# The last three c-rows of w_down: two loads of 96 partitions and five small ones in place of two loads of 128

## The chip, the cores and the metric

The kernel runs on one core of a Trainium2 chip. The metric is the device time of one execution in microseconds; the number given is the median of several runs.

## What is computed

One decode step of a transformer block for a single token: a layer norm, grouped-query attention against a long cache (32 query heads, 4 key and value heads, 65536 cached positions, head size 128), a residual, then a second layer norm and a gated feed-forward layer (model width D = 1024, F = 3584), again with a residual. All tensors are bfloat16.

```python
def _A_ref(x, k_cache, v_cache, wq, wo):
    q = (x @ wq)                      # 32 heads of 128
    scores = einsum(q, k) * Dh ** -0.5
    o = einsum(softmax(scores), v)
    return o @ wo
def _B_ref(x, w_gate, w_up, w_down):
    return (gelu(x @ w_gate) * (x @ w_up)) @ w_down
h  = x + _A_ref(layernorm(x), k_cache, v_cache, wq, wo)
h2 = h + _B_ref(layernorm(h), w_gate, w_up, w_down)
```

(cut: reshapes, transposes and the repeat of the key and value heads are left out.)

## The kernel before

The kernel reads some 173 MB once: the weights and the two caches. Everything is streamed through one large buffer in SBUF, `ring` (128 partitions, five chunks of 32 KB each per partition). `load` at L160 picks the next chunks and issues one DMA on SP's queue (L167); all large loads go this way, in the order of the program. The small input row x is loaded on ACT's queue at L172, four partitions of 512 bytes. SP waits before a load until the chunk it overwrites has been used. A later load can thus be queued on the DMA engines while earlier ones are still running.

The order of the loads is: wq (two), the 16 key and 8 value loads of the attention, wo (two), w_gate (one), w_up (two), and w_down (five). Helpers `pe`, `dv` and `ac` keep the order of the instructions on TensorE, VectorE and ScalarE as written; matmuls are all recorded under L145 or L147, which are lines of the helper `mm`.

The change touches the last stage. `w_down` (3584 x 1024) is seen as `wd_v`, 128 partitions of 28 rows c of 1024 values: partition p holds the rows 28p to 28p + 27 of the matrix, so c counts the rows inside a partition. The 28 c-rows are loaded in five pieces of `sizes = [14, 7, 4, 2, 1]` c-rows (L538), all side by side in `ring`, so that the last piece, 256 KB, is small. After each piece come its matmuls: for each c four (`out_mm`, L467), one for each quarter of the 1024 columns, with the padded activation column `actz[:, c, :]` as the stationary operand and 256 columns of the weights as the moving one, all summed into `f_ps`. Those four run in four column groups of TensorE. `keep_busy` (L543) adds matmuls into an unused bank between the pieces, 3, 2 and 1 after the first three.

```python
for sz, nb in zip(sizes, busy):
    at[0] = 0
    wv = load(wd_v[:, c0:c0 + sz, :], c0 * D)
    for cc in range(sz):
        c = c0 + cc
        out_mm(actz[:, c, :], lambda g: wv[:, cc, g * OW:(g + 1) * OW], False, c + 1 == FC)
```

At the end VectorE copies `f_ps` to `o_fin` as bfloat16 (L558), and SP stores it, four partitions of 512 bytes (L559).

Of the kernel before, what the change touches and what calls it, by code (L numbers as in the profile page):

```python
# [17 lines left out]
def kernel(  # L18
# [13 lines left out]
    nc = tc.nc  # L32
    P = 128
    D = A_x.shape[-1]
# [6 lines left out]
    FC = F // P  # L41
# [35 lines left out]
    ring = chpool.tile([P, NBUF * CW], BF16, name="ring")  # L77
# [80 lines left out]
    at = [0]  # L158

    def load(src, off=0):  # L160
        n, w = src.shape[1], src.shape[2]
        units = -(-(off + n * w) // CW)
        o = at[0] * CW + off
        assert o + n * w <= NBUF * CW
        at[0] = (at[0] + units) % NBUF
        tv = ring[:, o:o + n * w]
        nc.sync.dma_start(out=tv.rearrange("p (n w) -> p n w", w=w), in_=src)  # L167
        return tv.rearrange("p (n w) -> p n w", w=w)
# [23 lines left out]
    for bp in range(4):  # L192
        s0 = 64 * (bp // 2) + bp % 2
        nc.vector.tensor_copy(out=esel[:, bp, :, :],
                              in_=ident_bf[:, s0:s0 + 63:2].unsqueeze(1).to_broadcast([P, 4, 32]))
# [27 lines left out]
    def padded(pool, vec, ncols, name, tag=None):  # L223
        t = pool.tile([P, ncols, 32], BF16, name=name, tag=tag or name)
        nc.gpsimd.memset(t[:], 0.0)
        nc.vector.tensor_copy(out=t[:, :, 0], in_=vec)
        return t
# [228 lines left out]
    for wc in range(Hq // WN):  # L456
        wv = load(wo_v[:, wc * WN:(wc + 1) * WN, :])
        for cc in range(WN):
            c = wc * WN + cc
# [7 lines left out]
    def out_mm(stat, mov, first, last, groups=range(4)):  # L467
        for g in groups:
            mm(f_ps[32 * g:32 * g + 32, :], stat, mov(g), first, last, tile_position=(0, 32 * g),
               skip_group_check=True)  # L470
# [65 lines left out]

    wd_v = B_w_down.rearrange("(p c) n -> p c n", p=P)
    sizes = [14, 7, 4, 2, 1]  # L538
    assert sum(sizes) == FC
    actz = padded(rows, act_bf[:], FC, "actz")  # L540
    w_ps = row_bank("w_ps")

    def keep_busy(n, src):  # L543
        for _ in range(n):
            mm(w_ps[:], ident_bf[:], src, True, True)

    keep_busy(8, wu[:, 0, 0:512])
    busy = [3, 2, 1, 0, 0]
    c0 = 0
    for sz, nb in zip(sizes, busy):  # L550
        at[0] = 0
        wv = load(wd_v[:, c0:c0 + sz, :], c0 * D)
        for cc in range(sz):
            c = c0 + cc
            out_mm(actz[:, c, :], lambda g: wv[:, cc, g * OW:(g + 1) * OW], False, c + 1 == FC)
        c0 += sz
        keep_busy(nb, wv[:, 0, 0:512])
# [32 lines left out]
```

## Time and profile before

| what | value |
|---|---|
| median of 3 runs | 408.42 us (408.33 to 408.43) |
| span of the profiled execution | 406.9 us |
| DMA on SP's queue (q1) | 173.02 MB, 98.7% of 16 engines' span |
| bytes read, over the span | 173.02 MB, 425 GB/s |
| TensorE matmuls | 293.1 us busy, 72% |
| VectorE | 202.7 us busy, 50% |
| ScalarE, GpSimd | 44.7 us (11%), 7.4 us (2%) |
| mean granted TensorE clock | 0.912 |

The profiled execution's own time is its span, from the first to the last instruction of the core; the time of a run also has what lies around it, and the median of the runs is 1.5 us above the span. On a profile's page the rows of digits show the busy share in 40 equal slices, in tenths. In the chain that ended last each step is followed back to what released it. In a timeline, each row has the start and the duration in microseconds, the engine, the line of the kernel, the operation, out<-in, the shape and how many instructions were merged; the brackets give the idle time of the engine before them and what ended it. Names on DMA queues: q1 carries the kernel's loads from SP, q10 the load of x from ACT, q8 and q14 fetches of instructions.

### The profile page before, as it was taken

What the parts mean: (1) busy time and instruction counts of PE and PEld (TensorE: products, weight loads), DVE (VectorE), ACT (ScalarE), POOL (GpSimd) and SP (SyncE); (2) the same over time, 40 slices, a digit from 0 to 9 for tenths busy, and PEclk for the clock granted to TensorE, in tenths of its full rate; (3) what the DMA queues carried; (4) which work ended last, traced back from release to release, by engine and by line L of the source; (5) the groups of instructions that cost most, each with busy time, mean ns of one, the idle gap of its engine ahead of it and who ended that gap; (6) DMA issues with size and microseconds to landing.
All of it is one profiled execution on the core that took longest, in us unless ns stands there. A gap on an engine that the chain in (4) does not pass through costs nothing.

```text
span 406.9 us, 2667 instructions
## 1 busy us (share of the span) xinstructions
PE 293.1 (72%) x1495; PEld 60.8 (15%) x743; DVE 202.7 (50%) x185; ACT 44.7 (11%) x67; POOL 7.4 (2%) x17
## 2 busy tenths in 40 slices
PE   1346777769977699597776979976597969636283
PEld 0011111111111112111110111111111101212031
DVE  1118899955978359147971880879433000220110
ACT  1010000022000040100000420000041000100000
POOL 2000000000000000000000000000100000100000
PEclk9986899987989999899996998999989899886889
DMA  9999999999999999999999999999999999999995
GB/s 367 457 412 448 427 419 461 413 444 424 415 464 419 409 499 414 393 438 425 490 414 403 448 425 435 417 457 432 445 438 432 433 399 435 445 436 414 437 419 222
DMA packets 5213, 173.19 MB, mean 426 GB/s; under 512 B 585, under 2 KB 593, under 8 KB 849
## 3 DMA queue, kind: packets, MB, share of 16 engines
q1 hardware_dynamic: 5192, 173.02, 98.7%
q8 instruction: 9, 0.15, 0.1%
q14 instruction: 4, 0.02, 0.0%
q10 hardware_dynamic: 8, 0.00, 0.0%
HBM read 173.02 MB, written 0.00 MB: 425 GB/s over the span
## 4 chain that ended last, share of the span: by engine, by line
DMA 53%; PE 31%; DVE 12%; ACT 2%; issue 0%; SPq 0%; ACTq 0%
DMA ring<-in_A_v_cache_dram 31%; PE acc_ps L147 11%; DVE ring L281 9%; PE qk_ps L145 7%; DMA ring<-in_A_k_cache_dram 7%; DMA ring<-in_B_w_down_dram 7%; DMA ring<-in_B_w_gate_dram 7%; PE qk_ps L147 7%; PE acc_ps L145 4%; DVE mx L302 2%; ACT sc L301 2%; PE wg_ps L145 0%; PE wg_ps L147 0%; DVE pT L330 0%; ACT pe_r L327 0%
## 5 line engine op out<-in xcount | busy, mean ns | idle before, releaser
L281 DVE STREAM_TRANSPOSE ring<-ring 128x2048 uint32<-128x2048 uint32 x64 | 142.7, 2280 | 33.6 <-DMA ring<-in_A_k_cache_dram 33.5
L145 PE MATMUL qk_ps<-ring,wsel 128*128 128x512 bf16 x256 | 100.8, 394 | 35.8 <-DVE mx L302 23.6
L147 PE MATMUL acc_ps<-ring,pT 128*128 128x512 bf16 x384 | 114.1, 409 | 0.0
L147 PE MATMUL qk_ps<-ring,wsel 128*128 128x512 bf16 x256 | 100.6, 393 | 0.0
L145 PE MATMUL acc_ps<-ring,pT 128*128 128x512 bf16 x128 | 52.7, 412 | 20.4 <-DMA ring<-in_A_v_cache_dram 17.6
L145 PEld LDWEIGHTS <-wsel 128*128 128x128 bf16 x256 | 25.4, 99 | 135.1 <-issue 134.4
L301 ACT COPY sc<-qk_ps 128x1024 f32<-128x1024 f32 x16 | 16.2, 1011 | 176.8 <-PE qk_ps L147 176.7
L302 DVE TENSOR_REDUCE mx<-qk_ps 128x1 f32<-128x1024 f32 x16 | 19.6, 1222 | 26.0 <-ACT sc L301 26.0
L145 PEld LDWEIGHTS <-pT 128*128 128x128 bf16 x128 | 13.3, 104 | 119.1 <-issue 113.2
L357 DVE COPY acc_sb<-acc_ps 32x512 f32<-32x512 f32 x8 | 5.4, 672 | 36.6 <-PE acc_ps L147 36.6
L327 ACT ACTIVATE pe_r<-sc,nbias 128x1024 bf16<-128x1024 f32 x16 | 18.2, 1140 | 39.2 <-DVE nbias L322 38.5
L330 DVE STREAM_TRANSPOSE pT<-pe_r 128x1024 bf16<-128x1024 bf16 x16 | 19.0, 1226 | 6.2 <-ACT pe_r L327 6.2
L359 ACT COPY acc_sb<-acc_ps 32x512 f32<-32x512 f32 x8 | 4.6, 577 | 65.0 <-DVE acc_sb L357 65.0
L145 PE MATMUL q_ps<-ring,xnz 128*32 128x512 bf16 x32 | 5.2, 623 | 7.9 <-DMA ring<-in_A_wq_dram 7.9
L145 PE MATMUL wu_ps<-ring,hnz 128*32 128x512 bf16 x32 | 4.7, 503 | 7.8 <-DMA ring<-in_B_w_up_dram 7.8
L145 PE MATMUL wg_ps<-ring,hnz 128*32 128x512 bf16 x32 | 4.6, 517 | 7.7 <-DMA ring<-in_B_w_gate_dram 7.7
L145 PE MATMUL ln_tot<-ln_s,ones_f 128*128 128x1 f32 x8 | 1.9, 312 | 10.8 <-DVE ln_s L199 9.0
L315 DVE TENSOR_REDUCE gm<-mxT_ps 1x8 f32<-1x128 f32 x4 | 1.1, 279 | 16.1 <-PE mxT_ps L156 16.1
L145 PE MATMUL o_ps<-sel,acc_sb 128*128 128x8 f32 x32 | 4.2, 257 | 6.5 <-DVE rl L371 5.7
L145 PE MATMUL f_ps<-ring,actz 128*32 128x256 bf16 x112 | 4.0, 274 | 4.8 <-DMA ring<-in_B_w_down_dram 4.8
L237 DVE COPY q_ev<-q_ps 128x512 f32<-128x512 f32 x1 | 0.7, 692 | 13.3 <-PE q_ps L147 13.3
L237 DVE COPY wg_ev<-wg_ps 128x512 f32<-128x512 f32 x1 | 0.7, 691 | 11.6 <-PE wg_ps L145 11.6
(103 smaller groups left out, 89.2 us busy)
## 6 DMA issues: line engine op xcount, KB each, us to landing
ring<-in_A_k_cache_dram SPq DMA_DIRECT2D x16, 4096.0 KB, 33.9
ring<-in_A_wq_dram SPq DMA_DIRECT2D x2, 4096.0 KB, 16.5
ring<-in_A_wo_dram SPq DMA_DIRECT2D x2, 4096.0 KB, 30.8
ring<-in_B_w_gate_dram SPq DMA_DIRECT2D x1, 7168.0 KB
ring<-in_B_w_up_dram SPq DMA_DIRECT2D x2, 3584.0 KB, 30.5
ring<-in_B_w_down_dram SPq DMA_DIRECT2D x1, 3584.0 KB, 37.1
ring<-in_B_w_down_dram SPq DMA_DIRECT2D x1, 1792.0 KB
ring<-in_B_w_down_dram SPq DMA_DIRECT2D x1, 1024.0 KB, 29.3
```

Source lines behind the costliest of these rows:

```text
L145: return pe(t.matmul(out, lhsT=lhsT, rhs=rhs, start=start, stop=stop, tile_position=tile_position, skip_group_check=skip_group_check))
L147: op = t.add_instruction(mybir.InstMatmult(name=nc.get_next_instruction_name(), engine=t.engine, start_tensor_calc=start, stop_tensor_calc ...
L237: nc.vector.tensor_copy(out=dst, in_=src)
L281: dv(nc.vector.transpose(out=kt[:, c * w:(c + 1) * w], in_=kt[:, c * w:(c + 1) * w]))
L301: ac(nc.scalar.copy(out=sc[:], in_=flat))
L302: dv(nc.vector.tensor_reduce(out=state[("mx", g)][:, li:li + 1], in_=flat, axis=AX.X, op=ALU.max))
L315: dv(nc.vector.tensor_reduce(out=gm[:], in_=mxT_ps[:].rearrange("o (x h) -> o h x", h=rep), axis=AX.X, op=ALU.max))
L327: ac(nc.scalar.activation(out=pe_r[:], in_=state.pop(("sc", g, li))[:], func=ACT.Exp, bias=nbias[:, 0:1], scale=scale, accum_out=lpart[:, ...
L330: dv(nc.vector.transpose(out=pT[:].rearrange("p m c -> p (m c)"), in_=pe_r[:]))
L357: dv(nc.vector.tensor_copy(out=acc_sb[sl, :], in_=acc[sl, c, :]))
L359: ac(nc.scalar.copy(out=acc_sb[sl, :], in_=acc[sl, c, :]))
```

## The change

The first three loads of w_down (14, 7 and 4 c-rows) stay. The last two (2 and 1 c-rows) are cut to the partitions 0 to 95. The partitions 96 to 127 get their last three c-rows together, 6 KB a partition, in five loads of 12, 8, 6, 4 and 2 partitions. All ten loads are issued ahead of the first matmul of the stage in the program; the matmuls, their order and `keep_busy` stay. The places in `ring` stay the same too. The matmuls of the last two pieces read all 128 partitions, so they now depend on the five small loads also.

```diff
-    assert sum(sizes) == FC
+    shared = [96, 96]
+    extra = [12, 8, 6, 4, 2]
+    assert sum(sizes) == FC and 96 + sum(extra) == P
...
     c0 = 0
+    wd_s = ring[:, 0:FC * D].rearrange("p (c n) -> p c n", n=D)
+    ends = FC - sum(sizes[3:])
+
+    def wd_load(p0, p1, ca, cb):
+        nc.sync.dma_start(out=wd_s[p0:p1, ca:cb, :], in_=wd_v[p0:p1, ca:cb, :])
+
+    for sz, rows_in in zip(sizes, [P, P, P] + shared):
+        wd_load(0, rows_in, c0, c0 + sz)
+        c0 += sz
+    p0 = shared[0]
+    for n in extra:
+        wd_load(p0, p0 + n, ends, FC)
+        p0 += n
+    c0 = 0
     for sz, nb in zip(sizes, busy):
-        at[0] = 0
-        wv = load(wd_v[:, c0:c0 + sz, :], c0 * D)
+        wv = wd_s[:, c0:c0 + sz, :]
```

## The prediction

> **What bounds the kernel now.** I read the page first: which resource is full, and what the chain that ended last is made of.
>
> ```profile
> DMA  9999999999999999999999999999999999999995
> DMA 53%; PE 31%; DVE 12%; ACT 2%; issue 0%; SPq 0%; ACTq 0%
> q1 hardware_dynamic: 5192, 173.02, 98.7%
> q8 instruction: 9, 0.15, 0.1%
> q14 instruction: 4, 0.02, 0.0%
> ```
>
> The loads on q1 keep the 16 DMA engines busy for 98.7% of the span; PE and DVE steps of the chain lie beside loads that are under way. So the end is set by the last bytes of the last loads, and by what follows them. The end of the merged chain of waits shows that tail:
>
> ```profile
> 373.51 29.95 DMA ring<-in_B_w_down_dram
> 403.51 0.32 PE f_ps L145 x4
> 403.85 0.42 DVE o_fin L558
> ```
>
> The last load is issued at 373.51 and lands just before 403.51; then four matmuls, one copy, the store. The timeline shows what each of the five w_down loads (14, 7, 4, 2, 1 rows of c) releases:
>
> ```profile
> 395.00 1.71 PE L145 MATMUL f_ps<-ring,actz 128*32 128x256 bf16 x56 [1.63 <-DMA ring<-in_B_w_down_dram]
> 399.24 0.95 PE L145 MATMUL f_ps<-ring,actz 128*32 128x256 bf16 x28 [1.78 <-DMA ring<-in_B_w_down_dram]
> 401.67 0.62 PE L145 MATMUL f_ps<-ring,actz 128*32 128x256 bf16 x16 [0.94 <-DMA ring<-in_B_w_down_dram]
> 402.89 0.40 PE L145 MATMUL f_ps<-ring,actz 128*32 128x256 bf16 x8 [0.28 <-DMA ring<-in_B_w_down_dram]
> 403.51 0.29 PE L145 MATMUL f_ps<-ring,actz 128*32 128x256 bf16 x4 [0.21 <-DMA ring<-in_B_w_down_dram]
> 404.30 0.66 SPq L559 DMA_DIRECT2D out_dram<-o_fin  x1
> ```
>
> Groups of 16, 8 and 4 take 0.62, 0.40 and 0.29 us: 0.0275 us for each matmul more. The eight of the fourth load are over before the fifth lands.
>
> **Which engine is late, and why.** The arrivals on the last load's semaphore, one for each DMA engine, run from 401.55 to 403.46: the engines end 1.9 us apart. The trace's packet records have start, duration and bytes, but no engine. They can still be followed: on one engine the next packet starts 4 ns before the recorded end of the last, and every engine has the same list of sizes. Followed this way, the records fall into sixteen complete chains. Their last markers (4 bytes, some 0.32 us before the arrival) lie at: four chains at 401.22, 401.44, 401.53 and 401.81, without any fetch of code; eight at 402.51 to 403.14, with one 16 KB fetch each (the q8 line: eight of its nine fetches fall in before the end); and four that also carried the four-row load of x at the start, at 401.32, 401.39, 402.11 (one 8 KB fetch of q14) and 403.06 (two such fetches). A 16 KB fetch sets its engine back by some 1.4 us (955 ns of its own, and 481 more for the packet beside it, 1694 instead of 1213), an 8 KB fetch by 0.84 us (309 + 530).
>
> So there is something to even out: the mean of the sixteen ends is 402.35, the last 403.14.
>
> **The change, part by part.** Packets of 2, 4 and 8 KB follow each other at 80, 155 and 306 ns, so one of 6 KB costs some 230, and 236 with its marker. Rows 0 to 95 in 16 equal shares are 6 rows instead of 8 for each engine: 2 x (155 + 80) = 0.47 us less. Rows 96 to 127 then go one row to an engine: 12 + 8 + 6 + 4 + 2 = 32. The trace has one load of few rows, that of x: four rows, four engines, four arrivals (6.92 to 7.04). I read from it that a load of n rows takes n engines, and that the same first ones come first. [...]
>
> At full pace the balance is then: engines with no extra row -0.47; one, -0.23; two, 0.00; three, +0.24; four, +0.47; five, +0.71. The four chains that carried x are the ones with four or five. One of these is the chain that ended at 403.06. It began its last three rows of c at 403.06 - 8 x 0.235 - 0.01 = 401.17; now it has 6 x 0.235 = 1.41 shared and 0.94 or 1.18 of extras, and ends at 403.52 or 403.76. The eight late chains go forward to 402.9 and below, for nothing: the last marker moves from 403.14 to 403.5 or 403.8, +0.38 or +0.62.
>
> What a packet costs where several engines write to few neighbouring rows, no row of the trace shows: every large load goes to 128 rows at once. Below, the bound is the same pace: packets from 2 to 64 KB all run at it, so I exclude a gain. Above, I take double, somewhat over the dearest sharing that the trace has: a fetch beside a load's packet makes 1694 of 1213 (x 1.40), and 955 of some 608 (x 1.57). I take x 1.4, the row that is nearest to two streams that meet: the small loads put up to twelve engines on twelve adjacent rows while the late engines still write there, and the shared ones 16 on 96. The late low engine then ends at 401.17 + 1.97 + 1.32 = 404.46 or + 1.65 = 404.79: +1.32 or +1.65. Doubled, it is 401.17 + 2.82 + 1.89 or 2.36 = 405.9 or 406.35.
>
> [...]
>
> **PE.** In the changed program's order the first weight load of the fourth group waits for all five small loads and the 96-row load with it. So 12 matmuls (0.51 us by the step of 0.0275) instead of 4 (0.29) follow the last landing: +0.22. Behind them stand only the copy and the store. Gaps of 1.63 and 0.21 us before a group leave the step per matmul the same, so a longer gap costs no pace. Waiting on six counters instead of one costs between 0 and 0.1 us; I take 0.
>
> **SP.** Five issues more, of 0.33 to 0.43 us, on a queue with nothing else left but the store: "SPq L559 <- DVE o_fin L558" waited 30.3 us. They reuse arrival counters, so the loads of 8, 6, 4 and 2 rows are issued only after the two w_up loads and the first two w_down loads have landed: 377.96, 386.41, 394.95 and 399.20. The store's first packet came 1.26 us after its issue began (404.30 to 405.56), so the two-row load can start at 400.5; the earliest low engine is free for it at 401.32 - 0.47 + 3 or 4 x 0.236 = 401.6 or later. Covered by 1.1 us; without that cover it would be added one for one.
>
> **Sum.** Against the profiled execution (span 406.9; the median of the runs, 408.42, is 1.5 above it, for what lies around the span): +1.32 or +1.65 from the last marker, +0.22 from PE: +1.5 to +1.9. Predicted: 408.42 + 1.7 = 410.1.
>
> **Rivals.**
> *Full pace.* Packets to few rows run as before. Then +0.38 or +0.62, and 0.22: 409.0 to 409.3. For it: the one pace of all packets. Against it: 32 rows in small loads is a layout that the trace doesn't have.
> *Not slower.* The low engine that ends late gets at most two of the five extra rows (n x 0.236 below 0.47), because small loads are dealt over other engines than x was. Then the last marker is a late chain with one extra row, 403.14 - 0.23 = 402.90, and with 0.22 of PE the sum is 408.4. The most that evening out could ever bring is 403.14 - 402.35 = 0.79, less 0.22: 407.85. From the trace: for it, that eight of the nine late ends belong to chains which x did not use; against it, the ninth.
> *Doubled packets.* +2.7 to +3.2 and 0.22: 411.4 to 411.9.
>
> **How the numbers follow.** Forecast, with sharing between 1.2 and 1.9 times: 0.50. Full pace: 0.27. Not slower: 0.18. Doubled or worse: 0.05. A difference of 0.2% (0.82 us, to 407.60 or 409.24) is about what a measurement of this kernel can tell from no change. Full pace lies half on each side of 409.24: 0.13 and 0.14. Of "not slower" 0.16 is within, 0.02 below, since even perfect balance gives only 0.57. So faster 0.02, same 0.29, slower 0.69. The range goes from 408.5, in the middle of the "not slower" case, to 411.6 in the doubled one; some 0.15 lies outside.
>
> **What would show it.** After the change: the four-matmul line is now part of a group of 12 that starts after 404; the arrivals of the 12-, 8-, 6-, 4- and 2-row loads show which is last (I expect that with 4 or 2 rows); 6 KB packets at 226 to 235 ns are the rival "full pace", 300 or more the forecast. Wrong would be: a last arrival below 403.4, or a two-row load whose packets stand idle after its issue.

## The result, and the profile after

The changed kernel takes 412.13 us (411.87 to 412.23, 4 runs) where the kernel before takes 408.43 (408.33 to 408.63, 4 runs). The ratio is 1.009, interval 1.0077 to 1.0103: slower by 3.7 us. The forecast was 410.1, its range ended at 411.6. The sign was right, the size was not.

The timeline of the changed kernel, from the third w_down piece on (start, duration, engine, line, what it did, in brackets what the engine waited for):

```profile
399.05 0.95 PE L145 MATMUL f_ps<-ring,actz 128*32 128x256 bf16 x28 [1.78 <-DMA ring<-in_B_w_down_dram]
403.44 1.05 PE L145 MATMUL f_ps<-ring,actz 128*32 128x256 bf16 x16 [2.90 <-DMA ring<-in_B_w_down_dram]
405.77 0.83 PE L145 MATMUL f_ps<-ring,actz 128*32 128x256 bf16 x12 [0.75 <-DMA ring<-in_B_w_down_dram]
406.65 0.42 DVE L573 CAST o_fin<-f_ps 97x256 bf16<-97x256 f32 x1 [14.20 <-PE f_ps L145]
407.11 0.62 SPq L574 DMA_DIRECT2D out_dram<-o_fin  x1
```

Two things are to be seen. The third piece, whose load the change did not touch, starts at 403.44 instead of 401.67. And the groups of 16 and 12 matmuls take 1.05 and 0.83 us, where 16 took 0.62 before. The table of stretches says why the matmuls are slow (start:end, length, busy time of PE, PEld, DVE, ACT and POOL, then the granted clock, the DMA share and GB/s):

```profile
400.00:403.40 3.40, 0.54 (x2) 0.14 (x3) 0.00 (x0) 0.00 (x0) 0.00 (x0) 0.78 0.85 201
403.40:405.70 2.30, 1.59 (x17) 0.69 (x17) 0.00 (x0) 0.00 (x0) 0.00 (x0) 0.50 0.18 69
405.70:406.70 1.00, 0.83 (x12) 0.33 (x12) 0.05 (x1) 0.00 (x0) 0.00 (x0) 0.50 0.08 16
```

TensorE stands nearly idle from 400.5 to 403.4, the granted clock falls to 0.50 at 401.9 and stays there to the end. Before it was 1.00 to the end; the first of these stretches was then

```profile
400.00:403.40 3.40, 2.08 (x35) 0.93 (x28) 0.00 (x0) 0.00 (x0) 0.00 (x0) 1.00 0.69 277
```

The end of the merged chain of waits shows which load is last:

```profile
394.78 10.95 DMA ring<-in_B_w_down_dram
405.77 0.85 PE f_ps L145 x11
406.65 0.42 DVE o_fin L573
```

The load issued at 394.78 is the one of four partitions. Its four arrivals are at 403.71, 403.88, 404.23 and 405.73; the two-partition load had landed at 404.40.

The span went from 406.9 to 410.3, by 3.40 us, and falls into these terms:

| term | before | after | difference |
|---|---|---|---|
| last arrival | 403.46 | 405.73 | +2.27 |
| from it to the start of the copy | 0.39 | 0.92 | +0.54 |
| copy to the issue of the store | 0.45 | 0.45 | 0.00 |
| issue of the store to the end | 2.65 | 3.24 | +0.59 |

(The profiled execution of before was one of the longer ones: other executions of it had spans from 406.3 to 407.2, and the changed kernel 410.1 to 410.4. So the medians lie 0.3 us further apart than these two spans.)

**Where the 2.27 us come from.** The packet records were followed as in the prediction. The chain that ended at 403.06 before, with two 8 KB fetches, is there again, and four 6 KB packets are on it:

| stage of that chain | packets | at the pace of before | measured |
|---|---|---|---|
| third load, 128 partitions | 8 x 8 KB | 2.45 | 4.17 (398.63 to 402.80) |
| two loads of 96 partitions | 6 x 4 KB, 6 x 2 KB | 1.41 | 1.56 (to 404.36) |
| small loads | 4 x 6 KB | 0.94 | 0.95 (to 405.31) |

Its new packets run almost at full pace. The 1.72 us go into its old ones. That is the third load, which goes to 128 partitions as before: six early engines are done with it between 399.15 and 399.55, and from then on they write 96-partition packets while ten others are still in it. The packets of 8 KB that start up to 399.44 all take 309 ns; the first slow one, 486 ns, starts at 399.53. The eight chains that carry a 16 KB fetch lose 0.6 to 1.0 us at the same place (3.02 to 3.48 instead of 2.45).

### The profile page after: what moved, and what is told of

Its sections match the earlier page's. It is cut to its first block, busy times and chain, and to the rows that moved or that the text cites. A ratio compares the mean times of both kernels' runs of the same rounds, so it can differ in the third digit from the quotient of the medians.

```text
span 410.3 us, 2675 instructions
## 1 busy us (share of the span) xinstructions
PE 296.0 (72%) x1495; PEld 62.8 (15%) x743; DVE 202.6 (49%) x185; ACT 44.7 (11%) x67; POOL 7.4 (2%) x17
## 4 chain that ended last, share of the span: by engine, by line
DMA 61%; PE 25%; DVE 11%; ACT 1%; issue 0%; SPq 0%; ACTq 0%; DVEq 0%
DMA ring<-in_A_v_cache_dram 40%; PE acc_ps L147 13%; DMA ring<-in_B_w_down_dram 11%; DMA ring<-in_A_k_cache_dram 10%; DVE ring L281 9%; PE acc_ps L145 5%; PE qk_ps L145 3%; PE qk_ps L147 3%; DVE mx L302 1%; ACT sc L301 1%; PE at_ps L145 1%; PE at_ps L147 1%; PE o_ps L145 1%; DVE acc_sb L357 0%; ACT acc_sb L359 0%
```

## The experiments

Theory P: what counts is where the rows land; packets to few adjacent partitions slow those that other engines are still writing beside them. Theory D: what counts is how many packets each engine gets, and each keeps its pace. The numbers by P are the author's estimates, and no run shows what they rest on; in the first expectation, 409.6 to 410.2 is P's time. The times of before stand beside each: 408.41 in the first four, 408.46 in the last three.

### The two loads of 96 partitions alone

```diff
-    for n in extra:
-        wd_load(p0, p0 + n, ends, FC)
-        p0 += n
```

> The two loads of 96 partitions stay, the five small loads are left out (the matmuls read what the ring held on partitions 96 to 127). [...] Time about 409.6 to 410.2. Theory D, the loss comes from how the extra rows are dealt (four or five of them to one late engine) and packets keep their pace: 0.47 less on every engine, last arrival about 403.0, time about 407.9 to 408.1.

410.49 us, ratio 1.0052 (1.0035 to 1.0069). With 192 KB less to load, the kernel is 2.1 us slower. The third load's last arrival, at 401.62 before, is at 403.06, that of the last 96-partition load at 404.33. The third piece starts late, as in the change:

```profile
403.10 1.04 PE L145 MATMUL f_ps<-ring,actz 128*32 128x256 bf16 x16 [2.81 <-DMA ring<-in_B_w_down_dram]
```

Theory D is off by 2.4 us and has the wrong sign. P has the sign right and the time 0.3 too low. In this execution too the clock was at 0.50, and the last 12 matmuls took 0.83 us.

### The 32 partitions in one load

```diff
-    extra = [12, 8, 6, 4, 2]
+    extra = [32]
```

> The five small loads become one load of 32 partitions (96 to 127), two rows to each of 16 engines: the bytes of every engine are those of before again, nothing is dealt unevenly. [...] Theory D: every engine ends as before, 403.5, and 12 matmuls instead of 4 follow: about 408.6.

411.26 us, ratio 1.0071 (1.0056 to 1.0086). Third load 403.50, last 96-partition load 404.86, the 32 partitions 405.31. Every engine carries the bytes that it had before the change, and still the end comes 1.85 us later. Dealing the rows out unevenly, 405.73 in the change, adds only some 0.4, or 0.6 when both are counted from the landing of the second load (399.01 in the change, 399.17 here).

### Small loads behind full ones, adjacent or spread

Both variants keep the five loads of 128 partitions and add the small loads, as bytes that nothing needs, into a buffer `scr`; one unused matmul waits for them ahead of the fourth piece. They differ in the destination only (the edit in short; the name `dst` stands for the expression in each variant):

```diff
-        wd_load(p0, p0 + n, ends, FC)
+        dst = scr[p0:p0 + n, :]              # adjacent
+        dst = scr[o:o + 4 * n - 3:4, :]      # spread, with o = 0, 1, 2, 3, 33 for the five loads
+        nc.sync.dma_start(out=dst.rearrange("p (c n) -> p c n", n=D), in_=wd_v[p0:p0 + n, ends:FC, :])
```

> The five loads on 128 partitions stay as before; the five small loads are issued behind them, as additional bytes into a buffer of their own at partitions 96 to 127, adjacent as in the change, and one matmul into the unused bank waits for them ahead of the 2-c-row piece. Theory P: the last 128-row load arrives at about 404.4 instead of 403.46, the last small one at about 405.1; time about 411. Theory D: the last 128-row load stays at 403.5, the last small load at about 404.4 (403.06 + 4 x 0.236 and the arrival); the same as the variant with spread rows, about 409.7.

> [...] Theory P: the last 128-row load at 403.5 to 403.7, the last small one at 404.4 to 404.6, packets of 6 KB near 234 ns, time about 409.7 to 410.0, about 1 us below the adjacent variant. Theory D: no difference from the adjacent variant.

Adjacent: 411.60 us, ratio 1.0075 (1.006 to 1.009). Spread: 410.84, ratio 1.0061 (1.0046 to 1.0076). The intervals of the ratios overlap, so the times alone don't decide; the packets do. The durations in ns of all packets of one size in the w_down stage (mean, and the longest):

| kernel | 8 KB | 4 KB | 2 KB | 6 KB |
|---|---|---|---|---|
| before | 309, 309 | 159, 159 | 84, 84 | |
| the change | 380, 906 | 241, 386 | 116, 261 | 327, 574 |
| 96 alone | 374, 854 | 214, 405 | 110, 251 | |
| 128 and adjacent | 309, 309 | 177, 307 | 99, 213 | 289, 442 |
| 128 and spread | 309, 309 | 159, 159 | 84, 84 | 234, 234 |

With the rows spread, every one of the 32 small packets takes 234 ns and no other packet is disturbed. With the same sources, sizes, engines and order, but adjacent destinations, they take 289 on the mean and slow the full loads beside them. The last full load lands at 404.03 and 403.15, the last small one at 404.63 and 404.04. So it is the destination. Which property of it counts is not separated: the adjacent rows are neighbours at partitions 96 to 127, the spread ones lie four apart between 0 and 44. No record names an engine, and why the place counts is not shown.

The two timelines from that landing on, adjacent first, then spread:

```profile
404.68 0.39 PE L145 MATMUL w_ps<-scr,ident_bf 128*128 128x512 bf16 x1 [2.50 <-DMA scr<-in_B_w_down_dram]
405.00 0.51 PE L145 MATMUL f_ps<-ring,actz 128*32 128x256 bf16 x12
```

```profile
404.08 0.61 PE L145 MATMUL w_ps<-scr,ident_bf 128*128 128x512 bf16 x1 [1.38 <-DMA scr<-in_B_w_down_dram]
404.62 0.83 PE L145 MATMUL f_ps<-ring,actz 128*32 128x256 bf16 x12
```

The profiled execution of the spread variant had the clock at 0.50 here, the adjacent one at 1.00. That takes back some 0.5 of the 0.6 us that its landing gained, and is why the expected 409.7 to 410.0 was missed: neither the clock nor the longer closing was in it. The clock was at 0.50 here although nothing came late: the third piece, spread and then adjacent, was

```profile
401.12 1.04 PE L145 MATMUL f_ps<-ring,actz 128*32 128x256 bf16 x16 [0.96 <-DMA ring<-in_B_w_down_dram]
401.23 0.62 PE L145 MATMUL f_ps<-ring,actz 128*32 128x256 bf16 x16 [0.94 <-DMA ring<-in_B_w_down_dram]
```

### The changed kernel with TensorE kept busy

```diff
-    busy = [3, 2, 1, 0, 0]
+    busy = [9, 14, 4, 0, 0]
```

> The changed kernel itself, beside the two others of this call on the same chip. Last arrival near 405.7, the 12 matmuls at half the granted clock (0.83 us), time 411.9 to 412.2.

> The change with 9, 14 and 4 unused matmuls behind the first three pieces instead of 3, 2 and 1, so that TensorE does not stand idle from 400.5 to 403.4. Theory C, the idle stretch that the late third piece leaves halves the granted clock and that costs time at the end: the clock stays at 1.00 to the end, the 12 matmuls take 0.51 us instead of 0.83, time 0.3 to 0.4 us below the changed kernel. Rival: the clock falls whatever TensorE does there, or the added matmuls delay the pieces; no gain, or a loss.

The change again: 411.97 us, ratio 1.0085 (1.007 to 1.01). Kept busy: 411.69, ratio 1.0079 (1.0064 to 1.0094), with all its runs (411.55 to 411.87) below all of the other (411.89 to 412.04). The table of stretches of the kernel kept busy:

```profile
400.00:403.40 3.40, 3.10 (x21) 1.49 (x26) 0.00 (x0) 0.00 (x0) 0.00 (x0) 1.00 0.88 211
403.40:405.70 2.30, 1.41 (x20) 0.56 (x13) 0.00 (x0) 0.00 (x0) 0.00 (x0) 1.00 0.22 75
405.70:406.70 1.00, 0.51 (x12) 0.23 (x11) 0.42 (x1) 0.00 (x0) 0.00 (x0) 1.00 0.00 0
```

The clock is 1.00 throughout and the 12 matmuls take 0.51 us. So some 0.3 us of the loss is the clock: 0.28 by the times, 0.32 by the 12 matmuls. That it fell because the third piece was late is not shown. In the traces the granted clock changes after multiples of 3.41 us, and where these steps lie in the stage differs from one execution to the next. These are the steps that end with the fall, in the change and in the spread variant:

```profile
398.51:401.92 3.41, 1.49 (x30) 0.87 (x30) 0.00 (x0) 0.00 (x0) 0.00 (x0) 1.00 1.02 290
397.35:400.75 3.40, 1.49 (x30) 0.87 (x30) 0.00 (x0) 0.00 (x0) 0.00 (x0) 1.00 0.98 408
```

TensorE was busy for 1.49 us in both, and in the spread variant the fall came before its third piece, which was on time, began. Ahead of the last matmuls the clock fell in all four profiles with a late third piece and no added matmuls, and in one of the four with a third piece on time. So a late piece may make the fall more likely, but the fall did not need it. What sets it off is not shown.

### The closing

```diff
+        if 0 <= i < 8:      # i counts the loads from the 21st on
+            nc.sync.dma_start(out=tiny[2 * i:2 * i + 2, :], in_=tiny_v[2 * i:2 * i + 2, 0, 0:64])
```

> The kernel before with eight loads of two partitions of 128 bytes, one behind each of eight loads of the stage of the value cache; the output does not use them. Eight shift the arrival counters by a whole turn, so the store has the same counter as before. From the issue of the store to the end it took 2.65 us before, 3.19 with five loads more on SP. Theory A, the closing is longer because SP's program is longer: 3.1 to 3.3 here, time near 409.0. Theory B, it is longer because the store has another counter, which SP waits for first: 2.65 here, time within 0.1 of the kernel before.

408.64 us, ratio 1.0001 (0.9992 to 1.0011), and 2.65 us from the issue of the store at 404.48 to the end, as theory B says; the time is 0.2 above before instead of 0.1, which the interval can't tell apart. But the records show that the counter is the smaller part. At the end SP waits for the arrival counters two at a time, one pair after the other. In the kernel before, in the variant with 96 partitions alone (2.64) and here the store has a counter in the third of five pairs; with five loads more it has one in the first. The waits that stand behind the landing of the store for that reason make some 0.14 of the 0.59 us. The other 0.45 are a pause (after: 409.03 to 409.48). It lies at one place of SP's program. Counted from the start of the trace, in all seven profiles with 80 or more records of SP a pause of 0.44 to 0.48 us stands ahead of the 80th, whatever that record is. The two with 79, before and 96 alone, have none. Five loads more bring the 80th record behind the landing of the store. With the eight tiny loads it comes earlier, and the pause is over (405.11 to 405.55) before the store has landed, so it costs nothing. With one load more, the 32 partitions in one, it comes late in the closing, which took 2.88. So theory A was right in kind: more loads on SP lengthened the closing where they brought the pause behind the landing (3.24 in the change, 2.88 with one load more), and this run hid it. What the pause is stays open.

## Why the prediction was right or wrong

- **What bounds the end, and which engine is late**: right. "Low" in the prediction are the four chains that carried x; the late one of them, with its two fetches, ends last after the change (before, it ended 0.08 ahead of the last one), and it got four extra rows, as one of the two values in the prediction had it. These cost 0.95 us, the 0.94 of full pace. That the small loads start at the engines that x used had been read from that one load; the four 6 KB packets on this chain bear it out.
- **The balance by rows** (0.47 us less for the shared part): wrong for 96 partitions. The shared part of this chain took 1.56, so 0.32 less and not 0.47, and for all the loads of 96 partitions alone the end moved back by 0.87 instead of forward.
- **The price of sharing, x 1.4**: the factor was near. 6 KB packets took 327 instead of 234 on the mean (1.40), 4 KB 241 instead of 159 (1.52), 2 KB 116 instead of 84 (1.38). The step that failed is the one that applied it: I charged it to the new packets of the late engine, 1.41 + 0.94, and left the third load at its old pace. It was the other way round: new packets +0.16, third load +1.72. With that the last marker came at 405.31 and not at 404.46 or 404.79. The sign that was to tell the forecast from full pace, 6 KB packets of 300 ns or more, came true on the mean, while the four on the chain that ends last took 234 each.
- **PE**: the eight matmuls more cost 0.22 at the full clock, as said. "A longer gap costs no pace" was a reading of one execution. In the change the clock halved and the group of 12 took 0.83 instead of 0.51; in the spread variant it halved with gaps of 1.39, 1.77 and 0.96 us, about those of before. The sum had the clock at nothing. The wait on more counters cost nothing, as taken: 0.04 from the last arrival to the matmuls (405.73 to 405.77), where it was 0.05 before (403.46 to 403.51).
- **SP**: the covered issue was right. SP's waits show the loads waiting for counters,

```profile
SPq L556 <- DMA ring<-in_B_w_down_dram: 12.2, 2, 8.2
SPq L556 <- DMA ring<-in_B_w_up_dram: 11.6, 2, 8.2
```

  and the two-partition load was not the last to land. But "nothing else left but the store" overlooked that the longer program, 85 records instead of 79, brings SP's pause behind the landing of the store, and that the store's counter moves: +0.59 in the closing, a term that was not in the sum.
- **Full pace** and **not slower** are refuted by 906 ns for an 8 KB packet and by the 96 partitions alone. **Doubled** gave nearly the right time for a wrong reason: no packet class doubled on the mean.

In sum, of the 2.0 us between forecast and result, 0.6 to 0.95 is the last arrival (+2.27 instead of +1.32 or +1.65), 0.3 the way from it to the copy, with the clock (+0.54 instead of +0.22), and 0.6 the closing; the rest is the 0.3 between spans and medians.

## What to carry to other kernels

Here loads to a block of adjacent partitions slowed full loads that other engines were still running: with 96 partitions, packets of 8 KB took 374 ns on the mean instead of 309, and with 12 and fewer, packets of 4 KB took 177 instead of 159. Rows four partitions apart slowed nothing (309 and 159). It began, at 399.53 in the change, where the engines were out of step, six of them done with the third load and ten still in it, which is just where one would like to deal bytes out anew. Before moving bytes between DMA engines, ask which partitions they land on, and price the loads that are in flight beside them. Cost TensorE's clock and the closing waits as terms of their own: here they made 0.3 and 0.6 of the 3.4 us.

## What had not been expected of the hardware

One 8 KB packet of an untouched load was stretched from 309 to 906 ns by loads queued behind that load on other engines. SP paused for 0.44 to 0.48 us ahead of its 80th record in every profile that has one; with five DMA issues more this pause stood in the closing and made 0.45 of its 0.59 us. And the granted clock of TensorE fell after a step of 3.41 us in which TensorE was busy for 1.49.
